# Shares of the second matmul around the passage from half to full groups, and nine blocks in halves

## The chip, the cores and the metric

One core of a Trainium2 chip. The metric is device time in microseconds (us) of one execution; lower is better. A difference counts as a change in kind if it is over 2%. The profile's span, from first to last instruction, is mostly about 1.7 us shorter than the measured time.

## The reference

A short causal convolution along the sequence with softmaxed weights for each head, then a two-layer network with a leaky ReLU:

```python
w = softmax(weight)                              # 8 heads x 7 taps
out[b, s] = sum_k w[head, k] * x_pad[b, s + k]   # x: 8 x 4096 x 192
h = out.reshape(32768, 192) @ w_in               # w_in: 192 x 2048
g = maximum(0.01 * h, h)
y = g @ w_out                                    # w_out: 2048 x 192
```

## The kernel before

Each of 32 blocks holds 512 positions of two batch rows, one in each half of the 128 partitions. A block is worked as two half groups of 256 positions or one full group of 512. VectorE does the convolution into `yt` one group ahead; TensorE multiplies by `w_in` into a hidden tile of two PSUM banks; ScalarE applies the leaky ReLU and thereby empties it into `g`; TensorE multiplies `g` by `w_out`, which lags behind by a backlog of "slots".

```python
NHALF = 7                                    # blocks worked in halves
psum_h = tile_pool(name="ph", bufs=2, PSUM)  # hidden tiles: two banks each, two of them
psum_o = tile_pool(name="po", bufs=4, PSUM)  # outputs of the second matmul
groups = [(b, h * HT, HT) for b in range(NHALF) for h in range(2)]
groups += [(b, 0, ST) for b in range(NHALF, NBLK)]

def mm1(grp, u):                             # one hidden tile and its activation
    ph = psum_h.tile([128, 2, ST], FP32)
    ...  # nf = 512/T features x 3 chunks x 2 halves of the partitions: matmuls of T columns
    nc.scalar.activation(out=g[blk][...], in_=ph, func=Prelu, alpha=0.01)

def mm2_slot(q):   # two matmuls of 192 columns, side by side in the two halves of the rows
    ...            # 16 slots fill one round of a pair of outputs, 16 more the other round
    if last and rnd == 0: seal_round(p, ins)      # round 2 waits for the copy made here
    if last and rnd == 1: evac_o(pair[0])

def evac_o(n):
    copy = nc.scalar.copy if b < NHALF else nc.vector.tensor_copy
    ...            # then the transfer to the output

for i, grp in enumerate(groups):
    steps = T // 64                          # 4 in a half group, 8 in a full one
    quota = (avail - slot) // steps
    ...
    for j in range(steps):
        for u in range(2 * j, 2 * j + 2):
            mm1(grp, u)                      # two hidden tiles
        ...                                  # conv of the next group (VectorE)
        for _ in range(quota):
            mm2_slot(slot); slot += 1
        ...                                  # loads and transposes of later blocks
    avail += 2 * T // 128 * NFC              # 64 slots a half group, 128 a full one
```

So half groups have 16 slots in each step, full groups too, but the first full group finds a backlog of one half group only: 64 slots, 8 in each of its eight steps.

Of the kernel before, what the change touches and what calls it, by code (L numbers as in the profile page):

```python
# [14 lines left out]
def kernel(  # L15
# [25 lines left out]
    NFC = F // 128  # L41
    NB = S // ST
    NBLK = (B // 2) * NB
    NHALF = 7
    RUN = 4
    NPEC = 2

# [14 lines left out]

    groups = [(b, h * HT, HT) for b in range(NHALF) for h in range(2)]
    groups += [(b, 0, ST) for b in range(NHALF, NBLK)]

# [18 lines left out]
    def transpose_x(blk):  # L84

        if blk >= NBLK:
            return
        rp, st = divmod(blk, NB)
        if st == 0:
            new_xt(rp)  # L90
        t = x_bf.pop(blk)
        for c in range(NCH):
            nc.sync.dma_start_transpose(
                out=xt[rp][:, c, HALO + st * ST : HALO + (st + 1) * ST].rearrange(
                    "p (s k) -> p s k", s=SUB
                ),
                in_=t[:, c, :, :, :].rearrange("p s e k -> p (s e k)"),
            )
# [41 lines left out]
    def transpose_first(q):  # L140
        ts = [
            psum_o.tile([128, HS, NCH, CH], BF16, name=f"ptr{i}", tag="po") for i in range(2)
        ]
        for s in range(HS):
            for c in range(NCH):
                for i in range(2):
                    ps = slice(i * CH, (i + 1) * CH)
                    if q in x_half:
                        nc.tensor.transpose(  # L149
                            out=ts[i][:, s, c, :],  # L150
                            in_=x_half[q][ps, c, s, :, :].rearrange("p e k -> p (e k)"),
                            identity=ident[ps, ps],
                        )
                        continue
                    for e in range(2):
                        nc.tensor.transpose(  # L156
                            out=ts[i][e * CH : (e + 1) * CH, s, c, :],
                            in_=x_rows[q][ps, e, s, c * CH : (c + 1) * CH],
                            identity=ident[ps, ps],
                        )  # L160
        ptr[q] = ts

    def evac_first(q, *copies):
        dst = xt[0][:, :, HALO + q * HT : HALO + (q + 1) * HT].rearrange(
            "p c (s i k) -> p i s c k", s=HS, i=2
        )
        for i, t in enumerate(ptr.pop(q)):
            copies[i](out=dst[:, i], in_=t)  # L168
# [4 lines left out]
    def conv_jobs(grp, chunks=range(NCH)):  # L173
        blk, t0, T = grp
        rp, st = divmod(blk, NB)
        if blk not in yt:
            yt[blk] = yt_pool.tile([128, NCH, ST], BF16, name="yt")
        y = yt[blk]
        jobs = []
        for c in chunks:  # L180
            for k in range(K):
                a = BASE + k + st * ST + t0
                src = xt[rp][:, c, a : a + T]
                dst = y[:, c, t0 : t0 + T]
                if k == 0:
                    jobs.append(
                        lambda s=src, d=dst, c=c: nc.vector.tensor_scalar_mul(  # L187
                            d, s, wk[:, c, 0:1]
                        )
                    )  # L190
                else:
                    jobs.append(
                        lambda s=src, d=dst, c=c, k=k: nc.vector.scalar_tensor_tensor(  # L193
                            out=d, in0=s, scalar=wk[:, c, k : k + 1], in1=d,
                            op0=mybir.AluOpType.mult, op1=mybir.AluOpType.add,
                        )
                    )
        return jobs

    def pe_conv_jobs(grp, c):  # L200


        blk, t0, T = grp
        acc = psum_o.tile([128, ST], FP32, name="acc", tag="po")
        jobs = []
        for p in range(2):
            for k in range(K):
                a = BASE + k + blk * ST + t0
                for e in range(2):
                    ps = slice(e * CH, (e + 1) * CH)  # L210
                    jobs.append(
                        lambda k=k, p=p, a=a, e=e, ps=ps: nc.tensor.matmul(  # L212
                            out=acc[ps, :T], lhsT=diag[c][ps, p, k, :],
                            rhs=xt[0][ps, c, a : a + T],
                            start=(k == 0 and p == 0), stop=(k == K - 1 and p == 1),
                        )
                    )
        return jobs, lambda scale: scale(yt[blk][:, c, t0 : t0 + T], acc[:, :T], rsum[:, c, :])
# [173 lines left out]
    def mm1(grp, u):  # L392
        blk, t0, T = grp
        y = yt[blk]
        nf = ST // T
        ph = psum_h.tile([128, 2, ST], FP32, name="ph", tag="ph")
        for i in range(nf):
            f = nf * u + i
            for c in range(NCH):
                for e in range(2):  # L400
                    ps = slice(e * CH, (e + 1) * CH)
                    nc.tensor.matmul(  # L402
                        out=ph[:, e, i * T : (i + 1) * T],
                        lhsT=w_in_of(f, ps, c),
                        rhs=y[ps, c, t0 : t0 + T],
                        start=(c == 0),
                        stop=(c == NCH - 1),
                    )
        act = nc.scalar.activation(  # L409
            out=g[blk][:, nf * u : nf * (u + 1), :, t0 : t0 + T],  # L410
            in_=ph.rearrange("p e (i t) -> p i e t", i=nf),
            func=mybir.ActivationFunctionType.Prelu, alpha=0.01,
        )
        return act
# [53 lines left out]
    def evac_o(n):  # L468
# [4 lines left out]
        o_sb = osb[n // 2]  # L473
        copy = nc.scalar.copy if b < NHALF else nc.vector.tensor_copy
        ins = copy(out=o_sb[:, n % 2, :], in_=po.pop(n))  # L475
# [10 lines left out]
            )  # L486
        return ins

    slot, avail = 0, 0
    for i, grp in enumerate(groups):  # L490
        blk, t0, T = grp
        steps = T // 64
        if t0 == 0:
            g[blk] = g_pool.tile([128, NFC, 2, ST], BF16, name="g", tag="g")
        quota = (avail - slot) // steps

        if i == 0:
            ahead = []
        else:
            ahead = conv_jobs(groups[i + 1]) if i + 1 < len(groups) else []  # L500
        per = -(-len(ahead) // steps)
        for j in range(steps):
            for u in range(2 * j, 2 * j + 2):
                mm1(grp, u)
                if i == 0 and u == 1:
                    transpose_first(1)
                    evac_first(1, nc.vector.tensor_copy, nc.vector.tensor_copy)
                    pe_ahead, evac_y = pe_conv_jobs(groups[1], 0)
                    ahead = conv_jobs(groups[1], range(1, NCH))
                    per = len(ahead)  # L510
                if i == 0 and u in (2, 5):

                    n = len(pe_ahead) // 2
                    for job in pe_ahead[(u - 2) // 3 * n : (u + 1) // 3 * n]:
                        job()
                if i == 0 and u == 5:
                    evac_y(act_scale)
                if i == 0 and u == 6:
                    transpose_first(2)
            if i == 1 and j == 3:  # L520
                transpose_first(3)
            jobs = ahead[per * j : per * (j + 1)]
            if T == ST:


                jobs = ahead[len(ahead) * j // steps : len(ahead) * (j + 1) // steps]
                for job in jobs:
                    job()
                jobs = []
            for _ in range(quota):  # L530
                mm2_slot(slot)
                slot += 1
            if i == 0 and j == 3:
                evac_first(2, nc.vector.tensor_copy, nc.vector.tensor_copy)
            if i == 2 and j == 1:
                transpose_x(2)
            for job in jobs:
                job()
            if i == 1 and j == 3:
                evac_first(3, nc.vector.tensor_copy, nc.vector.tensor_copy)  # L540

            last_half = t0 + T == ST
            if j == steps // 4 and last_half:
                load_x(blk + 3)
            if j == steps // 2 and last_half and blk > 0:
                transpose_x(blk + 2)
        avail += 2 * T // 128 * NFC
# [36 lines left out]
```

## Time and profile before

| | before |
|---|---|
| measured, median of the first 3 runs | 693.19 us (692.6 to 693.42) |
| span of the profiled run | 691.1 us |
| TensorE, share of the span with a matmul in flight | 99% |
| VectorE, ScalarE | 79%, 76% |

A TensorE that is busy for 99% is not at 99% of its peak, since the records of matmuls overlap in this view: those of 192 columns last 243 ns on average, and 32 of them follow each other in 1.32 us, 41 ns apart. What shows a loss is the distance between the starts of like groups of matmuls. The prediction reads them from the timeline of the kernel before. Its columns are start, duration, engine, line, operation, tile, shapes, count, and in brackets the idle time before; its tail is the last 128 matmuls. First, the first slot of the second matmul and the tail (the last 128 matmuls, which use all 128 rows), seen on the weight loads:

```profile
22.74 1.39 PEld L428 LDWEIGHTS <-g 64*128 64x128 bf16 x32
...
677.38 10.51 PEld L428 LDWEIGHTS <-g 128*128 128x128 bf16 x128 [0.16 <-issue]
```

The distance, 677.38 - 22.74 = **654.64 us**, is called the steady stretch below. Second, the conv of block 8 on VectorE, the group after the first full one:

```profile
170.41 0.35 DVE L187 TENSOR_SCALAR yt<-xt,wk 128x512 bf16<-128x512 bf16 x1
170.79 4.69 DVE L193 SCALAR_TENSOR_TENSOR yt<-xt,wk,yt 128x512 bf16<-128x512 bf16 x6
175.40 0.35 DVE L187 TENSOR_SCALAR yt<-xt,wk 128x512 bf16<-128x512 bf16 x1
```

The third and last chunk of block 8 began at 170.41 and ended near 175.4, where the next block's conv starts. TensorE began block 8 at 175.18 and reads the third chunk from about 0.43 us into the group (four matmuls come before it, a pair for each of the two earlier chunks), so from 175.61. The chunk was on time by 0.2 us at most (0.1 by the end of its last record, 175.48).

### The profile page before, as it was taken

The numbers are of one execution on the slowest core, as the hardware profiler recorded it, in microseconds if no ns is written. First come the engines' busy times: TensorE is split into PE (matmuls) and PEld (weight loads), VectorE is DVE, ScalarE is ACT, GpSimd is POOL, SyncE is SP. The second block draws the span as 40 slices with busy tenths as digits, with TensorE's granted clock in tenths as the row PEclk, the third lists the DMA queues.
The fourth block names the chain that finished last, engine by engine and source line by source line (L and its number), as shares of the span: only waits on it lengthen the run. The fifth ranks groups of instructions, "written<-read, shape, count | busy, mean of one in ns | idle before, by whom it ended". The sixth has DMA issues, their size and how long they took to land.

```text
span 691.1 us, 26558 instructions
## 1 busy us (share of the span) xinstructions
PE 684.8 (99%) x11998; PEld 596.9 (86%) x11998; DVE 546.4 (79%) x1025; ACT 521.9 (76%) x593; POOL 147.2 (21%) x206
## 2 busy tenths in 40 slices
PE   8999999999999999999999999999999999999998
PEld 6999999997888888888888888888888888888887
DVE  6999999997778787878787878877878878787812
ACT  6888888889877777777777777777777777777771
POOL 7822210222222111222202222112222012000000
DMA  9976645559465356565445656265565455222112
GB/s 150 119 92 94 83 68 82 70 76 94 64 88 82 67 87 68 73 93 81 73 70 78 76 82 93 62 79 75 78 83 77 75 79 66 67 59 59 49 42 64
DMA packets 184161, 53.82 MB, mean 78 GB/s; under 512 B 149104, under 2 KB 183664, under 8 KB 184048
## 3 DMA queue, kind: packets, MB, share of 16 engines
q0 software_dynamic: 99536, 14.76, 30.6%
q1 hardware_dynamic: 84512, 37.38, 22.3%
q8 instruction: 93, 1.52, 1.0%
q14 instruction: 20, 0.16, 0.1%
HBM read 29.88 MB, written 25.17 MB: 80 GB/s over the span
## 4 chain that ended last, share of the span: by engine, by line
PE 96%; DMA 1%; ACT 1%; POOL 1%; issue 0%; DVE 0%; POOLq 0%
PE po L428 49%; PE ph L402 47%; DMA w_in<-in_moe_w_in_dram 1%; ACT g L409 1%; POOL w_in L248 0%; POOL x_rows L123 0%; PE acc L212 0%; POOL sel L233 0%; DVE o_sb L475 0%; PE ptr L156 0%; POOL ident masks.py:199 0%; POOL sel L231 0%; POOL ident masks.py:197 0%; PE ptr L149 0%; POOLq masks.py:199 0%
## 5 line engine op out<-in xcount | busy, mean ns | idle before, releaser
L409 ACT ACTIVATE g<-ph 128x1024 bf16<-128x1024 f32 x512 | 496.4, 1021 | 148.5 <-PE ph L402 148.1
L193 DVE SCALAR_TENSOR_TENSOR yt<-xt,wk,yt 128x512 bf16<-128x512 bf16 (+1 forms) x684 | 450.5, 659 | 19.4
L428 PE MATMUL po<-w_out,g 64*128 64x192 bf16 (+1 forms) x8064 | 388.1, 243 | 0.0
L428 PEld LDWEIGHTS <-g 64*128 64x128 bf16 (+1 forms) x8064 | 362.1, 94 | 29.5 <-issue 0.2
L402 PE MATMUL ph<-yt,w_in 64*128 64x512 bf16 (+1 forms) x3744 | 384.9, 338 | 2.2 <-DMA w_in<-in_moe_w_in_dram 1.2
L402 PEld LDWEIGHTS <-w_in 64*128 64x128 bf16 x3744 | 240.6, 111 | 56.8 <-issue 3.2
L78 POOL DMA_DIRECT2D x_bf<-in_x_dram x180 | 133.8, 776 | 425.8 <-DMA xt<-x_bf 423.2
L475 DVE COPY o_sb<-po 128x192 f32<-128x192 f32 x200 | 71.5, 358 | 113.7 <-PE po L428 108.0
L187 DVE TENSOR_SCALAR yt<-xt,wk 128x512 bf16<-128x512 bf16 (+1 forms) x114 | 39.6, 347 | 3.1 <-DMA xt<-x_bf 3.0
L475 ACT COPY o_sb<-po 128x192 f32<-128x192 f32 x56 | 17.9, 319 | 3.1 <-PE po L428 0.2
L282 PE MATMUL warm<-zero 128*128 128x256 bf16 (+1 forms) x22 | 5.2, 393 | 1.1 <-DVE junk L228 1.1
L212 PE MATMUL acc<-xt,diag 64*64 64x256 bf16 x84 | 5.7, 282 | 0.0
L212 PEld LDWEIGHTS <-diag 64*64 64x64 bf16 x84 | 4.5, 112 | 1.2 <-DVE wk L362 0.4
L127 POOL DMA_DIRECT2D x_half<-in_x_dram x6 | 4.3, 721 | 3.8 <-DMA w_in<-in_moe_w_in_dram 3.8
L168 DVE COPY xt<-ptr 128x384 bf16<-128x384 bf16 x7 | 2.2, 353 | 3.1 <-PE ptr L156 2.7
L282 PEld LDWEIGHTS <-zero 128*128 128x128 bf16 x22 | 2.6, 132 | 2.3 <-DVE junk L228 1.1
L248 POOL DMA_DIRECT2D w_in<-in_moe_w_in_dram x6 | 3.9, 658 | 0.0
L343 ACT ACTIVATE diag<-ident,whm 128x64 bf16<-128x64 bf16 x14 | 3.5, 337 | 0.0
L123 POOL DMA_DIRECT2D x_rows<-in_x_dram x4 | 2.9, 734 | 0.4 <-DMA w_in<-in_moe_w_in_dram 0.4
L368 ACT ACTIVATE yt<-acc,rsum 128x256 bf16<-128x256 f32 x3 | 1.4, 470 | 1.0 <-PE acc L212 1.0
L133 ACT CAST x_half<-x_nat 128x384 bf16<-128x384 f32 x2 | 1.0, 512 | 1.2 <-DMA x_nat<-in_x_dram 1.1
L288 ACT ACT_TABLE_LOAD x1 | 1.3, 1283 | 0.8 <-PEq L568 0.8
(37 smaller groups left out, 12.0 us busy)
## 6 DMA issues: line engine op xcount, KB each, us to landing
out_dram<-o_sb SPq DMA_DIRECT2D x117, 192.0 KB, 2.1
x_bf<-in_x_dram POOLq DMA_DIRECT2D x180, 64.0 KB, 3.4
out_dram<-o_sb SPq DMA_DIRECT2D x22, 96.0 KB, 1.6
xt<-x_bf SPq DMA_TRANSPOSE x90, 2.5
w_in<-in_moe_w_in_dram POOLq DMA_DIRECT2D x4, 192.0 KB, 5.5
w_in<-in_moe_w_in_dram POOLq DMA_DIRECT2D x2, 384.0 KB, 9.1
w_out<-in_moe_w_out_dram POOLq DMA_DIRECT2D x1, 768.0 KB, 11.9
x_nat<-in_x_dram SPq DMA_DIRECT2D x2, 192.0 KB, 2.6
```

The lines of the kernel that those rows point to most:

```text
L78: nc.gpsimd.dma_start(out=t[:, c, :, e, :], in_=src[2 * rp + e, :, :, c * CH : (c + 1) * CH],)
L127: nc.gpsimd.dma_start(out=x_half[q][:, c, :, e, :], in_=rows[:, e, :, c * CH : (c + 1) * CH],)
L187: lambda s=src, d=dst, c=c: nc.vector.tensor_scalar_mul(d, s, wk[:, c, 0:1])
L193: lambda s=src, d=dst, c=c, k=k: nc.vector.scalar_tensor_tensor(out=d, in0=s, scalar=wk[:, c, k : k + 1], in1=d, op0=mybir.AluOpType.mult, ...
L212: lambda k=k, p=p, a=a, e=e, ps=ps: nc.tensor.matmul(out=acc[ps, :T], lhsT=diag[c][ps, p, k, :], rhs=xt[0][ps, c, a : a + T], start=(k == ...
L248: nc.gpsimd.dma_start(out=w_in[n][e * CH : (e + 1) * CH], in_=moe_w_in[:, fs].rearrange("(c p) f -> p c f", p=CH),)
L282: nc.tensor.matmul(out=wa[:, 0, 0:cols], lhsT=zero[:, 0:128], rhs=zero[:, 0:cols], start=True, stop=True,)
L343: nc.scalar.activation(out=diag[c][:, 1, k, :], in_=ident2, func=mybir.ActivationFunctionType.Copy, scale=whm[:, c, 1, k : k + 1],)
L402: nc.tensor.matmul(out=ph[:, e, i * T : (i + 1) * T], lhsT=w_in_of(f, ps, c), rhs=y[ps, c, t0 : t0 + T], start=(c == 0), stop=(c == NCH - 1),)
L409: act = nc.scalar.activation(out=g[blk][:, nf * u : nf * (u + 1), :, t0 : t0 + T], in_=ph.rearrange("p e (i t) -> p i e t", i=nf), func=my ...
L428: return nc.tensor.matmul(out=po[m], lhsT=g[b][ps, fc, e, s * 128 : (s + 1) * 128], rhs=w_out[ps, fc, :], start=start, stop=stop,)
L475: ins = copy(out=o_sb[:, n % 2, :], in_=po.pop(n))
```

## The change

The intent is to smooth the passage from half to full groups. The last two half groups and the first full group shared their slots 64, 64, 64; now 48, 48, 96, in steps of 16 and 8, so that a round of 16 slots always ends with a step. And two more blocks are worked in halves.

```diff
-    NHALF = 7
+    NHALF = 9
...
+    plan = {
+        2 * NHALF - 2: [16, 8, 8, 16],
+        2 * NHALF - 1: [8, 8, 16, 16],
+        2 * NHALF: [16, 8, 8, 16, 8, 8, 16, 16],
+    }
...
-        quota = (avail - slot) // steps
+        quota = plan.get(i, [(avail - slot) // steps] * steps)
...
-            for _ in range(quota):
+            for _ in range(quota[j]):
```

## The prediction

> **What bounds the kernel now.** I read the page's head and chain first, then the waits, then the timeline around the place that the change touches, the passage from half groups (256 tokens) to full groups (512). The head, the busy shares, the chain by engine, and the costliest ScalarE group:
>
> ```profile
> span 691.1 us, 26558 instructions
> PE 684.8 (99%) x11998; PEld 596.9 (86%) x11998; DVE 546.4 (79%) x1025; ACT 521.9 (76%) x593; POOL 147.2 (21%) x206
> ...
> PE 96%; DMA 1%; ACT 1%; POOL 1%; issue 0%; DVE 0%; POOLq 0%
> ...
> L409 ACT ACTIVATE g<-ph 128x1024 bf16<-128x1024 f32 x512 | 496.4, 1021 | 148.5 <-PE ph L402 148.1
> ```
>
> The reader is to see that TensorE holds 96% of the chain that ends last and that its clock is full; ScalarE is idle 148.5 us before its activations, nearly all of it waiting for TensorE. So only TensorE's own work, or a place where another engine makes it wait, can move the time. Over the span the waits of TensorE for named work amount to 2.8 us, all before 23 us. That view misses one kind of stall, which shows only in the distance between starts of matmul groups. The timeline of the three kinds of step (columns: start, duration, engine, line, operation, tile, count, idle before). A step is two hidden tiles of the first matmul (L402), then a share of the second (L428):
>
> ```profile
> 140.06 1.50 PE L402 MATMUL ph<-yt,w_in 64*128 64x256 bf16 x24
> 142.69 1.50 PE L402 MATMUL ph<-yt,w_in 64*128 64x256 bf16 x24
> ...
> 158.47 1.49 PE L402 MATMUL ph<-yt,w_in 64*128 64x512 bf16 x12
> 159.35 3.89 ACT L409 ACTIVATE g<-ph 128x1024 bf16<-128x1024 f32 x4 [0.28 <-PE ph L402]
> 160.43 1.76 PE L402 MATMUL ph<-yt,w_in 64*128 64x512 bf16 x12
> 161.34 0.36 PEld L402 LDWEIGHTS <-w_in 64*128 64x128 bf16 x5 [0.37 <-issue]
> 162.65 1.49 PE L402 MATMUL ph<-yt,w_in 64*128 64x512 bf16 x12
> ...
> 175.18 1.50 PE L402 MATMUL ph<-yt,w_in 64*128 64x512 bf16 x12
> ...
> 177.79 1.50 PE L402 MATMUL ph<-yt,w_in 64*128 64x512 bf16 x12
> 180.41 1.50 PE L402 MATMUL ph<-yt,w_in 64*128 64x512 bf16 x12
> ```
>
> A half step of 16 slots takes 142.69 - 140.06 = 2.63 us, an ordinary full step 180.41 - 177.79 = 2.62 us. In the first full group (158.47 to 175.18, eight steps of 8 slots) they come in pairs: 1.96, then 2.22, so 4.18 for two, because in each second step the second hidden tile waits for ScalarE to empty its buffer (the matmul row grows from 1.49 to 1.76 us, and the weight loads split). Steps without a wait would take 8 x 1.96 = 15.68; the group takes 16.71. This is the whole loss there: **1.03 us**, in four stalls of about 0.26. It is what the change is after.
>
> The conv on VectorE runs just ahead of TensorE. Its three chunks for the first full group, and the start of the next group's conv, with the transposes that it waits for:
>
> ```profile
> 142.35 0.35 DVE L187 TENSOR_SCALAR yt<-xt,wk 128x512 bf16<-128x512 bf16 x1
> 147.34 0.35 DVE L187 TENSOR_SCALAR yt<-xt,wk 128x512 bf16<-128x512 bf16 x1
> 152.33 0.35 DVE L187 TENSOR_SCALAR yt<-xt,wk 128x512 bf16<-128x512 bf16 x1
> 156.90 4.64 SPq L93 DMA_TRANSPOSE xt<-x_bf  x3
> 160.43 0.36 DVE L187 TENSOR_SCALAR yt<-xt,wk 128x512 bf16<-128x512 bf16 x1 [3.02 <-DMA xt<-x_bf]
> ```
>
> That conv took 142.35 to 157.41 (160.43 less the wait of 3.02), and TensorE began the group at 158.47: a lead of only about 1.06 us. It is enough today, but the change shortens the two half groups in front of the first full one.
>
> **What the Trainium skill says.** "TensorE: Matmul & The Clock Gate", section "Wait — 56ns, not 53.3ns?", gives a fixed cost of about 2.5 ns on each warm matmul beside N columns at 2.4 GHz. Here two row tiles run side by side, so the unit is a pair ("TensorEngine Tiling (Array Packing)", section "Key Properties": tiles run matmuls in parallel). Estimates from that page: half step 12 x (106.7 + 2.5) + 16 x (80 + 2.5) = 2.630; full step 6 x (213.3 + 2.5) + 16 x 82.5 = 2.615. The trace agrees: starts from 45.38 to 155.84 are 42 half steps of 2.630, and from 177.79 to 653.72 are 182 full steps of 2.615. "Perfetto Trace Analysis", section "Matmuls", asks that matmul groups rotate through PSUM banks so that evacuation overlaps the next group. The hidden tile has two buffers of two banks, so that is done, but with a depth of two tiles, and the stalls above are where this depth is used up.
>
> **The change part by part.** *Two more blocks in halves.* Blocks 7 and 8 go from 2 x 8 full steps to 2 x 8 half steps. The columns are the same; 16 steps x 12 more matmuls = 192 more matmuls, that is 96 pairs x 2.5 ns = +0.24 us, all on the path (2.630 - 2.615 = 0.015 per step, x 16). The 16 more outputs of the second matmul copied by ScalarE and not VectorE (0.32 us each) lie in ScalarE's idle time: in a half step it already does such a copy and still waits 0.29 to 0.34 us.
>
> *The shares.* Before, the last two half groups and the first full one did 64 + 64 + 64 = 192 slots; after, 48 + 48 + 96 = 192. So the second matmul's work on TensorE does not change, and the backlog left afterwards is the same, 128 slots a full group from there on. What may change is the number of stalls. Before: eight steps of 8, in four pairs. After: 16,8,8,16 / 8,8,16,16 / 16,8,8,16,8,8,16,16 has again eight steps of 8 in four pairs, now each behind a step of 16. Does a step of 16 in front, in which ScalarE has spare time, save the pair its stall? I worked one pair from the trace's durations, with time 0 at the start of its first step. A hidden tile takes 0.65, its activation starts about 0.23 later, activations follow each other at 0.97, and the buffer is free about 0.05 after. First step: activations 0.88 to 1.85 and 1.85 to 2.82; it ends at 1.30 + 0.66 = 1.96. Second step: the first tile is done at 2.61, and its second tile needs the buffer that is free at 2.87. Wait 0.26, end 1.96 + 2.22 = 4.18. ScalarE was empty at time 0 in this working; spare time before cannot help, as it cannot start before the tile exists. The trace says the same: the first pair of before (158.47 to 162.65, 4.18) stands behind steps of 16 and stalls like the later ones. After the pair, the late output copy ends near 5.05, where the next step's first tile is due at 5.06, so the step of 16 is not delayed, and ScalarE has caught up at its end. So four stalls of about 0.26 remain: change of the sum about 0.0 (at most 0.1 gained).
>
> *Lead of VectorE.* In halves a conv chunk comes every 3.32 us (139.03 to 142.35), 9.97 a group, against 10.52 on TensorE: the lead grows 0.55 a half group, 2.2 us over four more. Against that, the two half groups with 48 slots last 9.46 and not 10.52, which takes 2.1 back. So the conv of the new first full group should end near 182.2 + 15.0 = 197.2, and TensorE should get there at 158.47 + 2 x 10.52 + 2 x 9.46 = 198.4: lead 1.2, as good as before. No stall, but without the two added blocks there would have been one of about 1 us; I take it that they are there for this.
>
> Sum: 0.24 - 0.02 = **+0.2 us**, on 693.19: 693.4.
>
> **The rivals.** (1) *The turn of 16 and 8 does remove the stalls*, because ScalarE averages out over 12 slots a step (1.30 + 12 x 0.0825 = 2.29 on TensorE against 1.94 + 0.22 on ScalarE). For it: on average TensorE is then the slower one, in eight equal steps of 8 it is not (1.96 against 2.09). Against it is the working above, which puts the stall down to the depth of the buffers and not to the average. It would make -1.03 + 0.24 = -0.8, so 692.4. (2) *VectorE or a transpose becomes late at the passage.* For it: a lead of 1.2 us is thin, and the conv of the group after waits for transposes (3.02 us in before). The order of instructions puts the transposes of block 10 behind the output transfer that follows the third step of the last half group, so by the rhythm of before (3.6 us from step to issue, 3.5 to landing) they land near 200.4, and the conv ends near 215.4; TensorE needs it at 198.4 + 18.8 = 217.2. A slip of 2 us or more there shows: +1 to +2, so 694.5 to 695.5. Against: every landing so far was 3 to 4 us after issue. (3) *Something in the slower half groups costs more than counted*, through ScalarE's copies of 16 more outputs: at most 16 x 0.32 = 5 us if none were hidden, 698; against it, 50 half steps already carry such a copy at 2.630.
>
> **Range and chances.** The three runs of before spread over 692.6 to 693.42, so 0.4 either way is noise. Rival 1 (I give it one in six) pulls to 692.4, rival 2 (one in ten) to 694.5 and above. That makes 693.4, with 692.4 to 694.4 to hold it 8 times in 10. Two per cent is 13.9 us; nothing here could gain a tenth of it, since the only loss touched is 1.03 us: faster 0.01. Slower would need a new recurring wait: 0.01. Within 2%: 0.98.
>
> **What would show each step.** In the changed kernel's timeline: on L402, 384 more matmuls of 256 columns in place of 192 of 512, in half steps of 2.630 up to block 7; four stalled steps of about 2.2 in the three planned groups, each behind one of 1.96 (my main step; if starts read 1.96, 1.96 there, rival 1 holds); no gap on TensorE at the start of block 9 or 10 (else rival 2); starts after the passage at 2.615 again, and the tail as before. Wrong would be any difference beyond 1.5 us either way, and above all one that lies outside blocks 7 to 10.

## The result

| | before | after |
|---|---|---|
| measured, median of 6 runs | 693.31 (692.6 to 695.51) | 693.22 (692.54 to 693.87) |
| ratio | | 0.9992 (95%: 0.9976 to 1.0008) |
| profiled span | 691.1 | 690.8 |
| steady stretch | 654.64 | 654.85 |

Ratios are the mean time of one kernel's fast runs over that of the other's of the same rounds, so not quite the ratio of the medians. By the clock on the wall nothing changed. The steady stretch is 0.21 us longer. From the page of the kernel after:

```profile
span 690.8 us, 26984 instructions
PE 685.0 (99%) x12190; PEld 600.9 (87%) x12190; DVE 550.4 (80%) x1051; ACT 527.0 (76%) x609; POOL 147.2 (21%) x206
...
PE 96%; DMA 1%; ACT 1%; POOL 1%; issue 0%; DVE 0%; POOLq 0%
```

TensorE holds the same 96% of the chain, with 12190 - 11998 = 192 more matmuls. ScalarE is 5.1 us busier (527.0 against 521.9) for the 16 more output copies; that nobody waits for them is shown by e6_halves21 below. The timeline of the kernel after, weight loads of the first slot and of the tail:

```profile
22.28 1.39 PEld L428 LDWEIGHTS <-g 64*128 64x128 bf16 x32
...
677.13 10.51 PEld L428 LDWEIGHTS <-g 128*128 128x128 bf16 x128 [0.16 <-issue]
```

677.13 - 22.28 = 654.85; the shorter span comes from the start, where the first slot came 0.46 us sooner. The timeline of the kernel after in the first planned group, and at the start of the first full one:

```profile
181.69 1.50 PE L402 MATMUL ph<-yt,w_in 64*128 64x256 bf16 x24
...
183.66 1.75 PE L402 MATMUL ph<-yt,w_in 64*128 64x256 bf16 x24
184.56 0.58 PEld L402 LDWEIGHTS <-w_in 64*128 64x128 bf16 x11 [0.25 <-issue]
...
185.87 1.51 PE L402 MATMUL ph<-yt,w_in 64*128 64x256 bf16 x24
...
188.50 1.51 PE L402 MATMUL ph<-yt,w_in 64*128 64x256 bf16 x24
...
197.95 1.49 PE L402 MATMUL ph<-yt,w_in 64*128 64x512 bf16 x12
```

The step at 181.69 takes 1.97, that at 183.66 takes 2.21 with the matmul row drawn out to 1.75, and the step of 16 after them an ordinary 2.63. All four pairs of short steps in the three planned groups look so. The four stalls of 0.26 are still there, each in the second step of a pair that stands behind a step of 16. What VectorE did meanwhile (timeline of the kernel after):

```profile
196.38 4.66 SPq L93 DMA_TRANSPOSE xt<-x_bf  x3
...
198.93 0.35 DVE L187 TENSOR_SCALAR yt<-xt,wk 128x512 bf16<-128x512 bf16 x1 [1.38 <-DMA xt<-x_bf]
...
213.93 0.35 DVE L187 TENSOR_SCALAR yt<-xt,wk 128x512 bf16<-128x512 bf16 x1
...
216.77 1.49 PE L402 MATMUL ph<-yt,w_in 64*128 64x512 bf16 x12
```

The conv of block 9 ended at 198.93 - 1.38 = 197.55, and TensorE came at 197.95. The conv of block 10 ended near 213.93, and TensorE began the block at 216.77 and wanted the third chunk at 217.20: 3.3 us to spare, where before had 0.2 at the same place.

### The profile page after: what moved, and what is told of

Same layout as the page of the kernel before. It is cut to its first block, busy times and chain, and to the rows that moved or that the text cites. A ratio compares the mean times of both kernels' runs of the same rounds, so it can differ in the third digit from the quotient of the medians.

```text
span 690.8 us, 26984 instructions
## 1 busy us (share of the span) xinstructions
PE 685.0 (99%) x12190; PEld 600.9 (87%) x12190; DVE 550.4 (80%) x1051; ACT 527.0 (76%) x609; POOL 147.2 (21%) x206
## 4 chain that ended last, share of the span: by engine, by line
PE 96%; DMA 1%; ACT 1%; POOL 1%; issue 0%; DVE 0%; POOLq 0%
PE po L428 49%; PE ph L402 47%; DMA w_in<-in_moe_w_in_dram 1%; ACT g L409 1%; POOL w_in L248 0%; POOL x_rows L123 0%; PE acc L212 0%; POOL sel L233 0%; DVE o_sb L475 0%; PE ptr L156 0%; POOL ident masks.py:199 0%; POOL sel L231 0%; POOL ident masks.py:197 0%; PE ptr L149 0%; POOLq masks.py:199 0%
## 5 line engine op out<-in xcount | busy, mean ns | idle before, releaser
L193 DVE SCALAR_TENSOR_TENSOR yt<-xt,wk,yt 128x512 bf16<-128x512 bf16 (+1 forms) x720 | 458.3, 637 | 21.1
L402 PEld LDWEIGHTS <-w_in 64*128 64x128 bf16 x3936 | 246.1, 111 | 53.7 <-issue 3.0
L475 DVE COPY o_sb<-po 128x192 f32<-128x192 f32 x184 | 65.7, 357 | 109.4 <-PE po L428 100.6
L187 DVE TENSOR_SCALAR yt<-xt,wk 128x512 bf16<-128x512 bf16 (+1 forms) x120 | 41.0, 341 | 1.5 <-DMA xt<-x_bf 1.4
L475 ACT COPY o_sb<-po 128x192 f32<-128x192 f32 x72 | 23.0, 319 | 3.9 <-PE po L428 0.2
```

Source lines behind the costliest of these rows:

```text
L187: lambda s=src, d=dst, c=c: nc.vector.tensor_scalar_mul(d, s, wk[:, c, 0:1])
L193: lambda s=src, d=dst, c=c, k=k: nc.vector.scalar_tensor_tensor(out=d, in0=s, scalar=wk[:, c, k : k + 1], in1=d, op0=mybir.AluOpType.mult, ...
L402: nc.tensor.matmul(out=ph[:, e, i * T : (i + 1) * T], lhsT=w_in_of(f, ps, c), rhs=y[ps, c, t0 : t0 + T], start=(c == 0), stop=(c == NCH - 1),)
L475: ins = copy(out=o_sb[:, n % 2, :], in_=po.pop(n))
```

## The experiments

All kernels gave right results. In each table row the steady stretch comes from the timeline of that kernel, read as above; it resolves a tenth of a microsecond, which the measured times do not. Two profiles are an exception: e7_copy_before and e9_lead lost 0.45 and 0.39 us at 42 to 43 us to a late conv of the start-up, far from what was edited. In the other ten, every step outside the passage has its ordinary length from 35 us on.

| run | measured median (its before) | ratio, 95% | steady stretch | against before |
|---|---|---|---|---|
| e0_after_again | 693.65 (693.50) | 1.0001, 0.9988 to 1.0014 | 654.86 | +0.22 |
| e1_plan_only | 694.63 (693.50) | 1.0018, 1.0001 to 1.0035 | 655.84 | +1.20 |
| e2_halves_only | 693.93 (693.50) | 1.0002, 0.9988 to 1.0016 | 655.33 | +0.69 |
| e3_split | 693.50 (693.50) | 0.9997, 0.9984 to 1.0011 | 655.11 | +0.47 |
| e4_split_before | 693.41, one run | | 655.12 | +0.48 |
| e5_twelve | 698.79, one run | | 658.91 | +4.27 |
| e6_halves21 | 694.48 (693.77) | 1.0012, 0.9996 to 1.0029 | 656.30 | +1.66 |
| e7_copy_before | 694.35, one run | | 656.03 | +1.39 |
| e8_split_copy_early | 693.35 (693.22) | 0.9997, 0.9983 to 1.0011 | 654.51 | -0.13 |
| e9_lead | 693.29 (693.49) | 0.9990, 0.9976 to 1.0004 | 654.57 | -0.07 |

**The changed kernel again.** No edit.

> The changed kernel once more, beside before and the next three on one chip. My theory (stalls are set by the depth of the hidden tile's two buffers; half groups cost 2.5 ns for each added pair of matmuls): +0.2 us on before from the first steady step to the tail, here as in the first profile. The rival (the turn of 16 and 8 lets ScalarE average out): -0.8. A third reading to look at: the runs of before reached 695.51 where the changed kernel's stayed under 693.9, so before might now and then lose 1 to 2 us at its thin lead (VectorE ended the conv of block 8 at 175.40, and the group began at 175.18); then before's times should scatter upwards again, and this kernel's should not.

The steady stretch repeats to 0.01 us in these two profiles of one kernel. The profiled run took 695.43 us, 2.9 more than the first profile of the same kernel, and the whole of it lies before the first slot. Its timeline:

```profile
17.67 1.65 PE L402 MATMUL ph<-yt,w_in 64*128 64x256 bf16 x23 [1.40 <-DMA w_in<-in_moe_w_in_dram]
...
25.10 1.39 PEld L428 LDWEIGHTS <-g 64*128 64x128 bf16 x32
```

TensorE waited 1.4 us there for a piece of `w_in` (2.1 in all, against 0.7 in the first profile), and by the view of stretches the granted clock was then 0.50 from 19 to 22 us. So the third reading, that only before scatters upwards, falls: this kernel scatters too, and at the start. Why before scattered is not shown, since no slower run of it was profiled.

**The planned shares alone.**

```diff
-    NHALF = 9
+    NHALF = 7
```

> The planned shares with seven blocks in halves as before. My theory: the two shortened half groups bring TensorE to the first full group 2.1 us sooner (near 156.35 in before's clock), while its conv still ends at 157.4; the third chunk is needed 0.43 us into the group, so TensorE waits 0.6 to 0.7 us for VectorE there, and the time is before plus 0.5 to 0.7. If the added halves are not there for VectorE's lead, there is no wait, and the time is before's (change 0.0). The rival of the averaging ScalarE says before minus 1.0.

TensorE waits at the first full group for the third chunk of its conv (timeline of e1_plan_only):

```profile
156.26 0.63 PE L402 MATMUL ph<-yt,w_in 64*128 64x512 bf16 x4
...
157.93 1.06 PE L402 MATMUL ph<-yt,w_in 64*128 64x512 bf16 x8 [1.03 <-DVE yt L193]
```

The chunk is wanted at 156.26 + 0.43 = 156.69 and the matmuls go on at 157.93: 1.24 us lost, against 0.6 to 0.7 expected, because this conv ended at 157.79 and not 157.4. The steady stretch is 1.20 longer than before's. This is the lead of VectorE used up by two half groups that are 1.06 shorter each; without the added halves the planned shares lose more than they could gain.

**The halves alone.**

```diff
 (before)
-    NHALF = 7
+    NHALF = 9
```

> Nine blocks in halves with the shares of before (16 a half step, 8 a step in the first full group). My theory: four stalls of 0.26 in the first full group as before, and +0.24 us for 192 more matmuls: before plus 0.2, the same as the changed kernel within 0.1 between the first steady step and the tail. The rival: the planned shares were what saved time, so this one should be 1.0 slower than the changed kernel.

It came 0.48 slower than the changed kernel, not within 0.1. The four stalls in the first full group are there as expected. What I had not expected stands at the next group, in the timeline of e2_halves_only:

```profile
199.33 5.27 SPq L93 DMA_TRANSPOSE xt<-x_bf  x3
...
203.30 0.35 DVE L187 TENSOR_SCALAR yt<-xt,wk 128x512 bf16<-128x512 bf16 x1 [5.05 <-DMA xt<-x_bf]
...
217.61 0.63 PE L402 MATMUL ph<-yt,w_in 64*128 64x512 bf16 x4
218.50 1.06 PE L402 MATMUL ph<-yt,w_in 64*128 64x512 bf16 x8 [0.25 <-DVE yt L193]
```

VectorE stood 5.05 us for the transposes of block 10, started at 203.30, and was late: the matmuls wanted its third chunk near 218.04 and got it at 218.50. With eight short steps the first full group lasts 16.71 us, and the next conv takes 15.1 from the landing of its transposes. In the changed kernel that group has 96 slots and lasts 216.77 - 197.95 = 18.82. So the shift of slots into the first full group does something after all: it gives the next conv 2.1 us more. A larger lead out of the half groups does not help, since VectorE waits for the transposes there.

A second thing differs at this place. The transposes, issued 1.6 us before the first full group begins in both kernels, landed 203.30 - 199.33 = 3.97 us after issue here and 198.93 - 196.38 = 2.55 in the changed kernel. The profiles divide the same way: 3.53 to 4.07 in the four with the old shares (before, e2_halves_only, e4_split_before, e7_copy_before), 2.52 to 2.55 in the five with shifted shares and nine or more blocks in halves (after, e0_after_again, e3_split, e5_twelve, e6_halves21). Why they land sooner is not shown, and no run separates the 2.1 us from the 1.4; by these numbers either alone would have covered the 0.46.

**Four slots behind each hidden tile.** In short steps only:

```diff
+            early = 4 if quota[j] == 8 else 0
             for u in range(2 * j, 2 * j + 2):
                 mm1(grp, u)
+                if u == 2 * j:
+                    for _ in range(early):
+                        mm2_slot(slot)
+                        slot += 1
...
-            for _ in range(quota[j]):
+            for _ in range(quota[j] - early):
```

> The changed kernel, with the eight slots of each short step put four behind the first hidden tile and four behind the second, and not eight behind both. The work is the same. My theory: the second tile of the next step then comes 2.94 us after the start of a pair, and its buffer is free at 2.88, so the four stalls of 0.26 go: 1.0 us less than the changed kernel between the first steady step and the tail, steps of 1.96 and 1.96, unless VectorE's conv of block 9 (0.4 to 0.8 us of slack) takes back up to 0.3. If ScalarE's rate and not the buffers' depth sets those steps (1.94 of activations and 0.2 to 0.3 of a copy in 1.96), the stall stays: pairs of about 4.18.

Half right. The pairs shrank to 3.94 (four times 0.98 to 0.99), but the step of 16 behind each grew (timeline of e3_split):

```profile
186.18 1.83 PE L402 MATMUL ph<-yt,w_in 64*128 64x256 bf16 x24
187.00 0.31 ACT L475 COPY o_sb<-po 128x192 f32<-128x192 f32 x1
187.16 0.58 PEld L402 LDWEIGHTS <-w_in 64*128 64x128 bf16 x11 [0.32 <-issue]
...
189.13 0.85 PE L402 MATMUL ph<-yt,w_in 64*128 64x256 bf16 x12
```

That step took 189.13 - 186.18 = 2.95, against 2.63. The stall had moved to the second tile of the following step, and ended 0.26 us worse over the four pairs. So the depth of the buffers was not the whole story, and the next two runs take the first full group of before apart, where eight short steps follow each other.

**Split slots in before.** The edit of e3_split, on before.

> Before, with the eight slots of each step of the first full group put four behind each hidden tile. The last run of this change (in the planned groups) kept its loss, so two causes are now open for the pairs of 1.96 and 2.22: the depth of the buffers (a tile can be filled again only 1.9 us after its filling began), or the rate of ScalarE (four activations at 0.97 and one copy at 0.29 are 4.18, just the length of a pair). Depth alone: the pair shrinks to 3.94. Rate: it stays at 4.17 to 4.18, spread otherwise over its tiles.

The eight steps took 175.49 - 158.60 = 16.89 us against 16.71: nothing gained. The stalls now stand where a copy on ScalarE is late (timeline of e4_split_before):

```profile
163.34 0.31 ACT L475 COPY o_sb<-po 128x192 f32<-128x192 f32 x1
...
163.70 0.28 PEld L428 LDWEIGHTS <-g 64*128 64x128 bf16 x8 [0.82 <-ACT o_sb L475]
```

The early slots of a new round must wait for the copy that seals the old one, and this copy is queued behind four activations. In the numbers this fits "rate". The whole stretch is 0.48 longer than before's: 0.18 of it in these eight steps, 0.29 in the step after them (2.91).

**The copies on VectorE.** In the first full group only:

```diff
 (before)
-        copy = nc.scalar.copy if b < NHALF else nc.vector.tensor_copy
+        copy = nc.scalar.copy if b < NHALF and i != 2 * NHALF else nc.vector.tensor_copy
```

> Before, with the four output copies in the first full group done by VectorE and not by ScalarE, the slots as before. Rate: with the copy gone, four activations take 3.89, so pairs fall to about 3.93. Depth: the second tile of each second step still waits for its buffer, pairs stay at 4.18, and ScalarE gets about 0.27 of idle time in each. On either reading VectorE ends the next conv later and TensorE waits 1 us or more for it at the start of block 8.

The pairs stay, which fits "depth" (timeline of e7_copy_before):

```profile
169.10 1.49 PE L402 MATMUL ph<-yt,w_in 64*128 64x512 bf16 x12
169.98 3.89 ACT L409 ACTIVATE g<-ph 128x1024 bf16<-128x1024 f32 x4 [0.28 <-PE ph L402]
...
171.06 1.75 PE L402 MATMUL ph<-yt,w_in 64*128 64x512 bf16 x12
...
173.27 1.49 PE L402 MATMUL ph<-yt,w_in 64*128 64x512 bf16 x12
```

From 169.10 to 173.27 is 4.17, with ScalarE now idle for 0.28 in each pair. Of the +1.39, two parts are made by VectorE: one step of the group waits for a copy (it takes 2.57 us), and block 8 starts 0.6 late. The last 0.45 is a late conv at an early step, at 42 us, which this edit does not touch.

Neither remedy helps alone: with the copy gone the buffers hold the pair at 4.17, with the buffers relieved the copy holds the group at 16.9. Each of the two is one profile, but the steps inside it repeat. That needed a run with both.

**Both, and earlier transposes.** The edits of e4_split_before and e7_copy_before, and:

```diff
-            if j == steps // 2 and last_half and blk > 0:
+            early_t = 3 <= blk < NHALF
+            if j == steps // 2 and (t0 == 0 if early_t else last_half) and blk > 0:
```

> Before with three things at once: four slots behind each hidden tile in the first full group (takes the depth away), the four copies there on VectorE (takes ScalarE's copy away), and the transposes of blocks 5 to 8 half a block sooner, so that VectorE can begin the conv of block 8 at once, near 157.4 and not 160.4, and can bear the copies. If depth and rate together made the stalls, pairs are 3.93 to 3.95, with up to 0.2 of a stall where the slots of the next pair of outputs wait for the copy on VectorE: 0.5 to 1.0 us less than before between the first steady step and the tail, and 692.5 to 693.0 measured, which is inside the scatter of the runs. If something else held TensorE there, nothing is gained.

The four stalls are gone. The eight steps take 174.05 - 158.34 = 15.71, just the 15.68 that before's durations gave for steps without a wait, and ScalarE runs 16 activations without a gap. But then (timeline of e8_split_copy_early):

```profile
159.22 15.73 ACT L409 ACTIVATE g<-ph 128x1024 bf16<-128x1024 f32 x16 [0.28 <-PE ph L402]
...
174.05 0.60 PE L402 MATMUL ph<-yt,w_in 64*128 64x512 bf16 x4
175.22 0.35 DVE L475 COPY o_sb<-po 128x192 f32<-128x192 f32 x1
175.35 1.06 PE L402 MATMUL ph<-yt,w_in 64*128 64x512 bf16 x8 [0.70 <-DVE yt L193]
```

VectorE's copies waited for TensorE in this trace (1.24, 0.31 and 0.21 us), with the rest of the conv behind them. What the third edit, the earlier transposes, did for the four stalls was not tested apart. Block 8's third chunk came late, its first step took 3.48 and not 2.62, and 0.86 of the 1.0 gained was given back.

**More lead for it.** The edits of e8_split_copy_early with `NHALF = 9`, and more of the conv ahead of the first copy:

```diff
+                cut = [len(ahead) * n // steps for n in range(steps + 1)]
+                if i == 2 * NHALF:
+                    cut = [0, 5, 9, 12, 14, 17, 19, 21, 21]
-                jobs = ahead[len(ahead) * j // steps : len(ahead) * (j + 1) // steps]
+                jobs = ahead[cut[j] : cut[j + 1]]
```

> The last run freed the first full group of its four stalls (15.71 us for eight steps, before 16.71), and gave 0.86 back at the start of the next block, because VectorE's conv was held up behind its own copies and came 0.7 late. This one keeps the split slots, the copies on VectorE and the early transposes, takes nine blocks in halves for 2.2 us more lead, and puts nine of the 21 conv instructions ahead of the first copy, then 5, 5 and 2. My theory: eight steps of 1.96, no stall at the next block, +0.24 for the 192 added matmuls: 0.7 to 0.8 less than before between the first steady step and the tail, the best so far; in measured time 0.1%, inside the scatter. If VectorE is too full for it (15.0 of conv and 1.4 of copies in 15.7), 0.3 to 0.6 comes back at block 10.

The group again takes 15.70 (201.44 to 217.14). Block 10 starts without a wait for VectorE, but its first step takes 220.06 - 217.14 = 2.92, a stall of 0.30 (timeline of e9_lead):

```profile
202.32 17.68 ACT L409 ACTIVATE g<-ph 128x1024 bf16<-128x1024 f32 x18 [0.29 <-PE ph L402]
...
217.14 1.79 PE L402 MATMUL ph<-yt,w_in 64*128 64x512 bf16 x12
```

The drawn-out row is the second hidden tile waiting for its buffer once more, at the change from even spacing back to two tiles in a row, while ScalarE runs through 18 activations without a gap. With 0.24 for the halves, and 0.39 that this run lost at 43 us to a late conv in the start-up, the sum is -1.0 + 0.30 + 0.24 + 0.39 = -0.07, as measured. Without the 0.39 it would be -0.46, still short of the -0.7 to -0.8 expected, and the 0.30 came back through the hidden tile and not through VectorE. A version that beats both kernels by more than their scatter was not found.

**Twelve slots in every step.**

```diff
-        2 * NHALF - 2: [16, 8, 8, 16],
-        2 * NHALF - 1: [8, 8, 16, 16],
-        2 * NHALF: [16, 8, 8, 16, 8, 8, 16, 16],
+        2 * NHALF - 2: [12] * 4,
+        2 * NHALF - 1: [12] * 4,
+        2 * NHALF: [12] * 8,
```

> The changed kernel with 12 slots in each of the 16 planned steps in place of 16 and 8 in turn, so the same 192 in all. The averages favour it (2.29 on TensorE against 2.16 on ScalarE, no stall by depth). But the two halves of a pair of outputs (16 slots each) then change over inside a step, where TensorE must wait for ScalarE's copy, which is queued behind that step's two activations. My theory: about 1.3 to 1.7 us of stall at such a change-over, some seven of them, so 9 to 12 us slower than the changed kernel. The plain averages: 1.0 us faster.

4.06 slower than the changed kernel (steady stretch), less than half of what I expected. The mechanism is the expected one (timeline of e5_twelve):

```profile
186.18 0.33 ACT L475 COPY o_sb<-po 128x192 f32<-128x192 f32 x1
...
186.56 0.83 PE L428 MATMUL po<-w_out,g 64*128 64x192 bf16 x16 [1.26 <-ACT o_sb L475]
```

But it struck in four steps, not seven, with 1.1 to 1.5 us each, 5.1 in all: those in which a pair of outputs changes from its first round to its second. The four steps in which a pair ends inside the step (slots 32, 64, 128 and 160 of the 192) cost nothing, since by the code the next pair starts in other buffers of `psum_o`, and neither do rounds that end with a step. The other steps took 2.28 to 2.31, as the averages say, and so the four stalls of 0.26 were indeed gone: 5.1 - 1.05 = 4.1. The plan's turn of 16 and 8 avoids this: it keeps the ends of rounds at the ends of steps.

**21 blocks in halves.**

```diff
-    NHALF = 9
+    NHALF = 21
```

> The changed kernel with 21 blocks in halves in place of nine, the planned shares moved along. My theory: twelve more blocks at 8 x 0.015 us each (96 more pairs of matmuls for two blocks at 2.5 ns) add 1.44 us between the first steady step and the tail, and the 96 more output copies on ScalarE cost nothing. If the copies or the wider conv did cost, it would be 5 us or more.

Steady stretch 656.30 - 654.85 = 1.45 over the changed kernel, 1.44 expected: 0.12 us a block. The 96 more copies on ScalarE cost nothing.

## Why the prediction was right

The predicted 693.4 stands against 693.22 measured, within 2% as said. That much was safe, as the prediction says itself: the only loss touched was 1.03 us of 693. That the two times agree to 0.2 is luck: measured time could not tell +0.2 from nothing, with runs of one kernel up to 3.6 us apart (e1_plan_only); the steady stretch could. In the prediction's sum the term -0.02 has no working; nothing hangs on it.

- **Two more blocks in halves, +0.24.** Right. The stretch grew by 0.21 and 0.22 in two profiles, and twelve further blocks added 1.45, which is 2.5 ns for each of 576 added pairs of matmuls.
- **The stalls stay, change about 0.** Right in size and place: four pairs of 1.97 and 2.21. Rival 1 is out: the step of 16 in front does not save a pair its stall. But the reason given was only part of it. The prediction put the stall "down to the depth of the buffers and not to the average". In the first full group of before, depth and ScalarE's queue (activations plus a copy) both hold the pair near 4.18: taking away one gained nothing (e4_split_before, e7_copy_before), both together, with earlier transposes, freed 1.0 us (e8_split_copy_early).
- **Lead of VectorE.** Right in kind, and shown by e1_plan_only, where the wait was 1.24 and not "about 1". The lead in the changed kernel was 0.4 us, not 1.2, and 0.3 in e0_after_again. The side that was mis-sized is VectorE's: counted from the first slot, TensorE reached the first full group as predicted (197.95 - 22.28 = 175.67 against 198.4 - 22.74 = 175.7), while the conv ended 0.8 us later (197.55 - 22.28 = 175.27 against 197.2 - 22.74 = 174.5). It was still in time.
- **What the shift of slots is good for.** Missed. The prediction saw no use in it for the time. It lengthens the first full group by 2.1 us, and the transposes for the next conv land 1.0 us sooner after the group's start than in before, so that this conv has 3.3 us to spare and not 0.2; without the shift, nine halves cost 0.69 (e2_halves_only). Rival 2 named the place, but as a danger of the change and not of the kernel before.
- **Rival 3**, a cost of ScalarE's added copies, is out by e6_halves21.

So the change adds 0.24 us of pair overhead, takes lead from VectorE at the first full group and gives it back through the halves, and leaves the 1.03 us of stalls that it was after: +0.21 us in all.

## What to carry to other kernels

When one stretch of a pipeline has a short share of filler work, ask what ends the wait there with everything else undone: here two causes of nearly the same length lay on top of each other, and experiments that removed one showed nothing. Count the slack of the engine that runs ahead at each change of group size, not only at the first. And where runs scatter by ten times the effect, compare a stretch inside the profile that leaves the start out.

## What the Trainium skill lacked or had wrong

- "TensorE: Matmul & The Clock Gate", section "Wait — 56ns, not 53.3ns?", gives the fixed 2.5 ns for a single matmul, and for matmuls packed side by side the span of one pack, not the spacing of packs in a stream. With two row tiles side by side the 2.5 ns come once for a pair: 1.45 us for 1152 added matmuls (e6_halves21 against the changed kernel), 2.5 ns for each of 576 pairs.
- "Perfetto Trace Analysis", section "Matmuls", asks for rotation through PSUM banks. It gives no way to size how deep; elsewhere the page only remarks that a repeating gap can mean too few buffers. Here a tile of 128x1024 was filled in 0.65 us, its activation began 0.23 later, and activations followed each other every 0.97. With two buffers TensorE stalled by 0.26 where two tiles in a row came every 1.96 us, also with ScalarE's copy taken away (e7_copy_before). Steps of 2.28 to 2.31 (e5_twelve) and of 2.62 showed no such stall.
- No page says that such a stall may leave no gap between the records of matmuls: TensorE's waits for the activation came to 0.2 us, at 22 us, with none of the four stalls of 0.26 among them; these stood only in the starts and as "issue" before weight loads (0.25 to 0.38).
- "TensorE: Matmul & The Clock Gate", section "Why this matters for your kernels", puts the idle gap to avoid at over about 3 us; for shorter, frequent ones the page gives no length. In e0_after_again waits of 0.7 and 1.4 us for weights during the start were followed by a granted clock of 0.50 from 19 to 22 us, and the first slot came 2.8 us later than in the first profile of the same kernel. That the one caused the other was not tested: e2_halves_only had 1.9 us of such waits in two pieces (1.1 the longer) and kept a clock of 1.00.
